# Reciprocals of the second MLP kept in SBUF, one block's input split later, keys split before queries

## The chip, the cores and the metric

The kernel runs on one core of a Trainium2 chip. The metric is the device time of one execution in microseconds (us). Runs of the kernel before are compared with runs of the changed kernel on the same chip.

## The reference, cut to what matters

An attention over 4 x 8 heads with 576 tokens and a head width of 64, masked by blocks of 64, is followed by two MLPs over 2304 tokens (model width 512, hidden width 2048):

```
x   = attention(q, k, v)                      # softmax over the blocks at or before one's own
x   = square(relu(x @ moe_w_in)) @ moe_w_out
h   = x @ moe2_w_in
P   = a[0] + a[1]*h + a[2]*h*h + a[3]*h*h*h
Q   = 1 + |b[0]|*|h| + |b[1]|*h*h
out = (P / (Q + 1e-6)) @ moe2_w_out
```

All arrays are float32.

## The kernel before, in words

**Precision.** TensorE multiplies in a rounded float32 format. Each factor is therefore kept as a high part (rounded) and a low part (the rest), and a product is three matmuls: high by high, low by high, high by low (PAIRS). High parts are written by a copy on ScalarE, low parts by a subtraction on VectorE or GpSimd (called POOL in the profile).

**Attention.** Heads 0 to 9 are multiplied plainly. Heads 10 to 31 are split: prep_qk (from line 249) runs one head ahead. In its first step ScalarE copies the scaled queries (qh, L259), then the keys (kk, L260). In the second step, one slot later, VectorE writes the queries' low part (L263, which reads qr and qh), POOL the keys' low part (L265, which reads kr and kk), and SP issues a DMA that copies the keys' high part to a second tile (L266). While the attention runs, TensorE fills in with the first half of the first MLP.

**First MLP.** Its hidden units are computed in halves; the second half of it runs after the attention, in units of one block of up to 512 tokens and 128 hidden columns.

**Second MLP** (from line 830). There are five blocks of tokens (512, 512, 512, 384, 384) and 16 slices of 128 hidden columns, so 80 units, 48 of width 512 and 32 of width 384. For unit u, TensorE multiplies x by a slice of w_in into a PSUM tile h (12 matmuls, L780; four such banks), and two units later g by a slice of w_out into the PSUM tiles yc (12 matmuls of 512 columns, 9 in the narrow blocks, L898), which are called down products here. Between them, with tiles t (three buffers), w and ab (two buffers each):

- ScalarE: ab = |h| (L878), w = c2*ab + c1 (L879), t = a3*h + a2 (L880)
- POOL: w = w*ab (L881); VectorE: t = h*t (L882), t = (t + a1)*h (L883)
- one unit later, ScalarE: ab = Ln of w (L862), r = Exp of -ab (L863), a first reciprocal of Q; VectorE: a Newton step and the product, w = (w + Q0)*r (L864), r = (2 - w)*r (L865), t = (t + a0)*r (L866)
- two units later, ScalarE writes g's high part from t (L857), POOL the low part (L858).

The tile r is chosen in L884: for the first two units (u < LAG) it is ab itself, in SBUF; for all others it is h, the PSUM tile of the unit, which is so read until L866. In the last two units VectorE takes POOL's part.

**What else runs there.** In units 0 to 9, split_late (L772 on ScalarE, L773 on POOL) splits the last ten of 16 late weight slices. The next block's x is split by split_x (L714 on ScalarE, L715 on POOL), in four pieces, at units 3, 5, 7 and 9 of a block.

**Order.** Tile's scheduler orders each engine's instructions when the kernel is built, by the program's order and a simulated timeline; on the chip each engine takes its queue in that order. tc.issue_after(x) ties what is issued in its block behind x on x's own engine. The lines that set the order around the change are these:

```
mid[u] = (ab, w, t, ab if u < LAG else h)                            # L884
if j + 1 < len(blocks3) and 3 <= m < 3 + 2 * KK and m % 2:           # L885
    with tc.issue_after(taken.ins), tc.issue_after(squared.ins):
        split_x(xt[j + 1], m // 2 - 1, blocks3[j + 1][1])
```

Of the kernel before, what the change touches and what calls it, by code (L numbers as in the profile page):

```python
# [11 lines left out]
AF = mybir.ActivationFunctionType  # L12
# [10 lines left out]
KK = DM // P  # L23
# [5 lines left out]
SCALE = 0.125  # L29
# [6 lines left out]
DOWN = 2.0 ** -63  # L36
# [8 lines left out]
def f(ap):  # L45
    return ap.bitcast(F32)
# [3 lines left out]
def attention_moe_moe(ctx: ExitStack, tc: tile.TileContext, q, k, v, wi1, wo1, wi2, wo2, a, b, out):  # L50
    nc = tc.nc
# [197 lines left out]
    def prep_qk(un, step):  # L249
        if un.plain:  # L250
            if step == 0 and un.scale == 1.0:
                cols = un.qr[:, un.q0:un.q1]
                nc.gpsimd.tensor_scalar(cols, cols, SCALE, 0.0, op0=ALU.mult, op1=ALU.add)
            return
        if step == 0:
            hd = un.hd
            un.qh = attn.tile([P, SP], F32R, tag="qh", name=f"qh{hd}", bufs=2)
            un.kk = attn.tile([P, S], F32R, tag="kk", name=f"kk{hd}", bufs=2)
            nc.scalar.activation(un.qh, un.qr, AF.Copy, scale=SCALE)  # L259
            nc.scalar.activation(un.kk, un.kr, AF.Copy)  # L260
        else:
            un.q2, un.k2 = q_two[un.hd % 2], k_two[un.hd % 2]
            nc.vector.scalar_tensor_tensor(  # L263
                un.q2[0:D], un.qr[0:D], SCALE, f(un.qh[0:D]), op0=ALU.mult, op1=ALU.subtract)
            nc.gpsimd.tensor_tensor(un.kk[D:P], un.kr[D:P], f(un.kk[D:P]), op=ALU.subtract)  # L265
            nc.sync.dma_start(f(un.k2[0:D]), f(un.kk[0:D]))  # L266
# [341 lines left out]
    lnb, exb = cab[:, 2:3], cab[:, 3:4]  # L608
# [35 lines left out]
    for i in range(NI + 5):  # L644
# [19 lines left out]
        if 0 <= i - 4 < NI:  # L664
            un, gi = slots[i - 4]
# [25 lines left out]
    def cut(small_first):  # L691
        tiles = NT // P
        nb = -(-tiles // (BLK // P))
        sizes = [P * (tiles // nb + (n < tiles % nb)) for n in range(nb)]
        cuts, t0 = [], 0
        for n in reversed(sizes) if small_first else sizes:
            cuts.append((t0, n))
            t0 += n
        return cuts

    blocks2, blocks3 = cut(True), cut(False)
# [10 lines left out]
    def split_x(xt, kk, n):  # L712
        hi, lo = xt[:, 0, kk, 0:n], xt[:, 1, kk, 0:n]
        nc.scalar.activation(hi, f(lo), AF.Copy)  # L714
        nc.gpsimd.tensor_tensor(lo, f(lo), f(hi), op=ALU.subtract)  # L715
# [69 lines left out]
    LAG = 2  # L785
# [5 lines left out]
    xt = {0: x_first}  # L791
    gs, ypart = {}, {}
    conv3.load()
    for u in range(len(units) + LAG):
        if u < len(units):
            j, m = units[u]
# [11 lines left out]
        if u >= LAG:  # L808
            j, m = units[u - LAG]
# [22 lines left out]
        at = u - (len(units) - HALF) - 1  # L832
# [10 lines left out]
    xt = {0: xt[len(blocks2)]}  # L843
    mid, gf = {}, {}
# [4 lines left out]
    for u in range(max(downs) + 1):  # L849
        if u - 2 in gf:  # L850
            t = gf.pop(u - 2)
            n = blocks3[units[u - 2][0]][1]
            if u - 2 >= final and (u - 2) % 7 > 2:
                g = half(len(blocks2) + len(blocks3))[:, :, (u - 2) % 7 - 3, 0:512]
            else:
                g = g2.tile([P, 2, 512], F32R, tag="g", name=f"gc{u - 2}", bufs=3)
            nc.scalar.activation(g[:, 0, 0:n], t, AF.Copy)  # L857
            (nc.vector if u - 2 >= len(units) - END else nc.gpsimd).tensor_tensor(g[:, 1, 0:n], t, f(g[:, 0, 0:n]), op=ALU.subtract)  # L858
            gs[u - 2] = g
        if u - 1 in mid:  # L860
            ab, w, t, r = mid.pop(u - 1)
            nc.scalar.activation(ab, w, AF.Ln, bias=lnb, scale=DOWN)  # L862
            nc.scalar.activation(r, ab, AF.Exp, bias=exb, scale=-1.0)  # L863
            nc.vector.scalar_tensor_tensor(w, w, Q0, r, op0=ALU.add, op1=ALU.mult)  # L864
            nc.vector.scalar_tensor_tensor(r, w, 2.0, r, op0=ALU.subtract, op1=ALU.mult, reverse0=True)  # L865
            nc.vector.scalar_tensor_tensor(t, t, a0, r, op0=ALU.add, op1=ALU.mult)  # L866
            gf[u - 1] = t
        split_late(u + len(blocks2) * HALF + LAG - SPLIT_AT, done)
        if u < len(units):
            j, m = units[u]  # L870
            t0, n = blocks3[j]
            if j + 1 < len(blocks3):
                if m == 0:
                    xt[j + 1] = load_x(xs2, *blocks3[j + 1], len(blocks2) + j + 1)
            ps = h_matmul(w3["i", m], xt[j], n, f"c{j}_{m}")
            h = ps[:, 0:n]
            ab, w, t = tmp("ab", n, f"ab{u}"), tmp("w", n, f"wq{u}"), tmp("t", n, f"t{u}")
            nc.scalar.activation(ab, h, AF.Abs)  # L878
            nc.scalar.activation(w, ab, AF.Identity, bias=c1, scale=c2)  # L879
            taken = nc.scalar.activation(t, h, AF.Identity, bias=a2, scale=a3)  # L880
            squared = (nc.vector if u >= len(units) - END else nc.gpsimd).tensor_tensor(w, w, ab, op=ALU.mult)  # L881
            nc.vector.tensor_tensor(t, h, t, op=ALU.mult)  # L882
            done = (taken, nc.vector.scalar_tensor_tensor(t, t, a1, h, op0=ALU.add, op1=ALU.mult))  # L883
            mid[u] = (ab, w, t, ab if u < LAG else h)  # L884
            if j + 1 < len(blocks3) and 3 <= m < 3 + 2 * KK and m % 2:  # L885
                with tc.issue_after(taken.ins), tc.issue_after(squared.ins):
                    split_x(xt[j + 1], m // 2 - 1, blocks3[j + 1][1])
        for v in downs.get(u, ()):
            j, m = units[v]
            t0, n = blocks3[j]  # L890
            g = gs.pop(v)
            for c in range(n // P):
                if m == 0:
                    acc[j, c] = psh.tile([P, 512], F32, tag="y", name=f"yc{j}_{c}", bufs=4)

                with tc.issue_after(last.ins) if c and v == len(units) - 1 else ExitStack():
                    for i, (zw, zg) in enumerate(PAIRS):
                        last = nc.tensor.matmul(acc[j, c], g[:, zg, P * c:P * (c + 1)], w3["o", m][:, zw, :],  # L898
                                                start=m == 0 and i == 0, stop=m == NM - 1 and i == 2)
                if m == NM - 1:  # L900
                    if c % 2 == 0:
                        o = g2.tile([P, 2, DM], F32, tag="wraw", name=f"o{j}_{c}", bufs=4)
                    y = acc.pop((j, c))
                    end_ = v == len(units) - 1 and c == n // P - 1
                    (nc.scalar.copy if c % 2 or end_ else nc.vector.tensor_copy)(o[:, c % 2], y)
                    if c % 2 or c == n // P - 1:
                        top = t0 + P * (c - c % 2)
                        (nc.scalar if end_ else nc.sync).dma_start(
                            out[top:t0 + P * (c + 1), :].rearrange("(a p) d -> p a d", p=P), o[:, 0:c % 2 + 1])
# [59 lines left out]
```

## Time and profile before

| | us |
|---|---|
| median of 3 runs | 1006.08 |
| lowest and highest of them | 1005.41, 1006.14 |
| the profiled execution | 1004.93 |
| its span, first to last instruction | 1003.2 |

The page of the profile gives, for the profiled execution, how long each engine was busy. PE is TensorE's matmul part, DVE is VectorE, ACT is ScalarE, SP issues DMAs. A time in the trace counts from the span's start. "Idle before" is how long the engine stood still ahead of an instruction, and the name behind "<-" is what it waited for. Lines are those of the kernel before. The time outside the span (1004.93 - 1003.2) belongs to no instruction.

### The profile page before, as it was taken

Reading aid. Unit: us, or ns where it says so; the run is one execution under the profiler, and the core shown is the slowest. Engines: PE = TensorE matmul, PEld = TensorE weight load, DVE = VectorE, ACT = ScalarE, POOL = GpSimd, SP = SyncE. Lnnn points to the kernel's source line nnn. Section 1 sums busy time; section 2 is a strip of 40 time slices with the busy share of each in tenths; the row PEclk is TensorE's granted clock in tenths of the full one; section 3 lists DMA queues with packets and bytes.
Section 4 is the critical chain, followed back from the end, with each engine's and each line's share of the span. In section 5 each row is a group of like instructions: output and inputs, shape, how many; then the busy total and the mean of one; then the engine's idle time right before and its main releaser. Section 6 shows DMA issues by size and latency. Waiting matters only on the chain.

```text
span 1003.2 us, 16323 instructions
## 1 busy us (share of the span) xinstructions
PE 992.0 (99%) x5361; PEld 864.6 (86%) x5361; DVE 724.8 (72%) x1389; ACT 723.8 (72%) x1590; POOL 570.5 (57%) x617
## 2 busy tenths in 40 slices
PE   8999999999999999999999999999999999999998
PEld 6678999888888899999888887888888888899997
DVE  7898687877787478767768766757666666666765
ACT  7888697887886467655455557867777777787885
POOL 5777597886787268421215386854655554555542
PEclk9999999999999999999999999999999999999999
DMA  9864334334332244569654651002001100200000
GB/s 295 267 198 149 114 113 132 89 106 130 105 107 83 97 131 124 207 184 300 230 191 151 231 157 58 1 1 84 1 1 32 42 1 1 74 1 1 32 1 32
DMA packets 63844, 106.67 MB, mean 106 GB/s; under 512 B 17040, under 2 KB 33424, under 8 KB 63760
## 3 DMA queue, kind: packets, MB, share of 16 engines
q1 hardware_dynamic: 63184, 105.05, 33.5%
q8 instruction: 42, 0.69, 0.3%
q10 hardware_dynamic: 576, 0.59, 0.2%
q14 instruction: 42, 0.34, 0.1%
HBM read 79.30 MB, written 23.07 MB: 102 GB/s over the span
## 4 chain that ended last, share of the span: by engine, by line
PE 91%; ACT 3%; DVE 2%; POOL 1%; DMA 1%; issue 1%; POOLq 0%; DVEq 0%; ACTq 0%; SPq 0%
PE yc L898 19%; PE hc L780 19%; PE hb L780 10%; PE yb L821 10%; PE ya L562 10%; PE ha L540 9%; PE tp L300 5%; PE pv L483 4%; PE sx L335 3%; PE sy L335 2%; PE pv L470 1%; DMA qr<-in_q_dram 1%; DMA raw_ai<-in_wi_dram 1%; POOL rb L387 0%; ACT p L371 0%
## 5 line engine op out<-in xcount | busy, mean ns | idle before, releaser
L780 PE MATMUL hc<-ring,w_ci 128*128 128x512 f32 (+1 forms) x960 | 210.2, 368 | 1.0 <-DVE t L866 1.0
L780 PEld LDWEIGHTS hc<-ring,w_ci 128*128 128x128 f32 x960 | 176.2, 188 | 27.0 <-DVE t L866 1.4
L898 PE MATMUL yc<-w_co,gc 128*128 128x512 f32 x792 | 191.7, 390 | 0.0
L898 PEld LDWEIGHTS yc<-w_co,gc 128*128 128x128 f32 x792 | 148.2, 188 | 29.3
L858 POOL TENSOR_TENSOR gc<-t,gc 128x512 fp32r<-128x512 f32 (+1 forms) x70 | 85.1, 1215 | 89.4 <-issue 61.0
L881 POOL TENSOR_TENSOR wq<-wq,ab 128x512 f32<-128x512 f32 (+1 forms) x78 | 92.8, 1190 | 75.0 <-ACT wq L879 74.7
L540 PE MATMUL ha<-ring,w_ai 128*128 128x512 f32 (+3 forms) x576 | 117.5, 348 | 0.5 <-DVE xp L487 0.5
L821 PE MATMUL yb<-gb,w_bo 128*128 128x512 f32 (+1 forms) x480 | 105.3, 367 | 0.0
L780 PE MATMUL hb<-ring,w_bi 128*128 128x512 f32 (+1 forms) x480 | 105.2, 367 | 0.0
L540 PEld LDWEIGHTS ha<-ring,w_ai 128*128 128x128 f32 x576 | 94.1, 189 | 11.3 <-issue 3.0
L715 POOL TENSOR_TENSOR ring<-ring 128x512 fp32r<-128x512 f32 (+1 forms) x40 | 52.4, 1311 | 88.0 <-ACT ring L714 83.2
L882 DVE TENSOR_TENSOR t<-hc,t 128x512 f32<-128x512 f32 (+1 forms) x80 | 50.9, 636 | 67.7 <-ACT t L880 67.7
L821 PEld LDWEIGHTS yb<-gb,w_bo 128*128 128x128 f32 x480 | 87.6, 188 | 11.4
L780 PEld LDWEIGHTS hb<-ring,w_bi 128*128 128x128 f32 x480 | 87.5, 188 | 11.1
L562 PE MATMUL ya<-gring,w_ao 128*128 128x352 f32 (+3 forms) x480 | 88.9, 331 | 0.0
L864 DVE SCALAR_TENSOR_TENSOR wq<-wq,hc 128x512 f32<-128x512 f32 (+1 forms) x78 | 49.3, 632 | 53.0 <-ACT hc L863 35.6
L300 PE MATMUL tp<-ident,p 128*128 128x128 f32 x480 | 82.1, 281 | 1.4 <-DVE stat L394 1.0
L562 PEld LDWEIGHTS ya<-gring,w_ao 128*128 128x128 f32 x480 | 75.9, 188 | 4.0 <-DVE s L578 0.2
L399 POOL TENSOR_SCALAR p<-p,stat 64x64 f32<-64x64 f32 (+4 forms) x110 | 60.3, 552 | 28.9 <-DVE stat L395 14.4
L443 DVE TENSOR_TENSOR pt<-tp,pt 128x128 fp32r<-128x128 f32 (+2 forms) x176 | 63.2, 391 | 18.6 <-ACT pt L441 11.9
L441 ACT ACTIVATE pt<-tp 128x128 fp32r<-128x128 f32 (+2 forms) x176 | 56.7, 365 | 19.3 <-PE tp L300 17.4
L878 ACT ACTIVATE ab<-hc 128x512 f32<-128x512 f32 (+1 forms) x80 | 44.2, 553 | 36.3 <-PE hc L780 36.0
(157 smaller groups left out, 2099.3 us busy)
## 6 DMA issues: line engine op xcount, KB each, us to landing
kr<-in_k_dram SPq DMA_DIRECT2D x32, 288.0 KB, 3.6
raw_ci<-in_wi_dram SPq DMA_DIRECT2D x16, 512.0 KB, 4.4
raw_co<-in_wo_dram SPq DMA_DIRECT2D x16, 512.0 KB, 4.0
qr<-in_q_dram SPq DMA_DIRECT2D x24, 320.0 KB, 3.2
ring<-xs SPq DMA_DIRECT2D x24, 256.0 KB, 4.2
raw_ai<-in_wi_dram SPq DMA_DIRECT2D x8, 512.0 KB, 5.2
raw_ao<-in_wo_dram SPq DMA_DIRECT2D x8, 512.0 KB, 4.6
raw_bi<-in_wi_dram SPq DMA_DIRECT2D x8, 512.0 KB, 3.9
```

The source lines that it names most:

```text
L300: yield nc.tensor.transpose(ps[:, P * n:P * (n + 1)], ptile(un, t)[:, P * c:P * (c + 1)], ident)
L399: nc.gpsimd.tensor_scalar(pv, pv, st[r:P, 6 + n:7 + n], 0.0, op0=ALU.mult, op1=ALU.add)
L441: nc.scalar.activation(high, src, AF.Copy)
L443: nc.vector.tensor_tensor(low, src, f(high), op=ALU.subtract)
L540: nc.tensor.matmul(ps[:, 0:n], w[:, zw, P * kk:P * (kk + 1)], ring[:, zx, kk, x0:x0 + n], start=i == 0, stop=i == 3 * KK - 1)
L562: nc.tensor.matmul(ps[c][:, 0:n], wA["o", m][:, zw, P * c:P * (c + 1)], gs[m][:, zg, 0:n], start=m == 0 and i == 0, stop=m == HALF - 1 and ...
L715: nc.gpsimd.tensor_tensor(lo, f(lo), f(hi), op=ALU.subtract)
L780: nc.tensor.matmul(ps[:, 0:n], w[:, zw, P * kk:P * (kk + 1)], xt[:, zx, kk, 0:n], start=i == 0, stop=i == 3 * KK - 1)
L821: nc.tensor.matmul(acc[j, c][:, 0:n], wB["o", m][:, zw, P * c:P * (c + 1)], g[:, zg, 0:n], start=m == 0 and i == 0, stop=last and i == 2)
L858: (nc.vector if u - 2 >= len(units) - END else nc.gpsimd).tensor_tensor(g[:, 1, 0:n], t, f(g[:, 0, 0:n]), op=ALU.subtract)
L881: squared = (nc.vector if u >= len(units) - END else nc.gpsimd).tensor_tensor(w, w, ab, op=ALU.mult)
L898: last = nc.tensor.matmul(acc[j, c], g[:, zg, P * c:P * (c + 1)], w3["o", m][:, zw, :], start=m == 0 and i == 0, stop=m == NM - 1 and i == 2)
```

## The change

It does three things. In prep_qk, ScalarE writes the keys' high part first and the queries' high part second, held in that order. In the second MLP, r is the ab tile in SBUF for all 80 units: Ln is written into it from w, Exp in place, and h is no longer written to. And the four splits of x for the second block move, within the first block, from units 3, 5, 7 and 9 to units 10 to 13; in later blocks they stay at 3, 5, 7 and 9.

```diff
--- before.py
+++ after.py
@@ -256,8 +256,9 @@
             hd = un.hd
             un.qh = attn.tile([P, SP], F32R, tag="qh", name=f"qh{hd}", bufs=2)
             un.kk = attn.tile([P, S], F32R, tag="kk", name=f"kk{hd}", bufs=2)
-            nc.scalar.activation(un.qh, un.qr, AF.Copy, scale=SCALE)
-            nc.scalar.activation(un.kk, un.kr, AF.Copy)
+            high = nc.scalar.activation(un.kk, un.kr, AF.Copy)
+            with tc.issue_after(high.ins):
+                nc.scalar.activation(un.qh, un.qr, AF.Copy, scale=SCALE)
         else:
             un.q2, un.k2 = q_two[un.hd % 2], k_two[un.hd % 2]
             nc.vector.scalar_tensor_tensor(
@@ -858,9 +859,9 @@
             (nc.vector if u - 2 >= len(units) - END else nc.gpsimd).tensor_tensor(g[:, 1, 0:n], t, f(g[:, 0, 0:n]), op=ALU.subtract)
             gs[u - 2] = g
         if u - 1 in mid:
-            ab, w, t, r = mid.pop(u - 1)
-            nc.scalar.activation(ab, w, AF.Ln, bias=lnb, scale=DOWN)
-            nc.scalar.activation(r, ab, AF.Exp, bias=exb, scale=-1.0)
+            r, w, t = mid.pop(u - 1)
+            nc.scalar.activation(r, w, AF.Ln, bias=lnb, scale=DOWN)
+            nc.scalar.activation(r, r, AF.Exp, bias=exb, scale=-1.0)
             nc.vector.scalar_tensor_tensor(w, w, Q0, r, op0=ALU.add, op1=ALU.mult)
             nc.vector.scalar_tensor_tensor(r, w, 2.0, r, op0=ALU.subtract, op1=ALU.mult, reverse0=True)
             nc.vector.scalar_tensor_tensor(t, t, a0, r, op0=ALU.add, op1=ALU.mult)
@@ -881,10 +882,11 @@
             squared = (nc.vector if u >= len(units) - END else nc.gpsimd).tensor_tensor(w, w, ab, op=ALU.mult)
             nc.vector.tensor_tensor(t, h, t, op=ALU.mult)
             done = (taken, nc.vector.scalar_tensor_tensor(t, t, a1, h, op0=ALU.add, op1=ALU.mult))
-            mid[u] = (ab, w, t, ab if u < LAG else h)
-            if j + 1 < len(blocks3) and 3 <= m < 3 + 2 * KK and m % 2:
+            mid[u] = (ab, w, t)
+            at = range(10, 14) if j == 0 else range(3, 11, 2)
+            if j + 1 < len(blocks3) and m in at:
                 with tc.issue_after(taken.ins), tc.issue_after(squared.ins):
-                    split_x(xt[j + 1], m // 2 - 1, blocks3[j + 1][1])
+                    split_x(xt[j + 1], at.index(m), blocks3[j + 1][1])
         for v in downs.get(u, ()):
             j, m = units[v]
             t0, n = blocks3[j]
```


## Rows read from the trace of the kernel before

**Rows 1.** The page, part 1: busy time, share and instructions of each engine.

```profile
PE 992.0 (99%) x5361; PEld 864.6 (86%) x5361; DVE 724.8 (72%) x1389; ACT 723.8 (72%) x1590; POOL 570.5 (57%) x617
```

**Rows 2.** Who waited for whom on PE: us in total, times, longest us.

```profile
PE tp L300 <- DVE stat L394: 1.0, 1, 1.0
PE hc L780 <- DVE t L866: 1.0, 1, 1.0
PE pv L483 <- ACT pt L441: 0.5, 2, 0.3
PE ha L540 <- DVE xp L487: 0.5, 1, 0.5
```

**Rows 3.** The chain of waits, two pieces: start us, us, what.

```profile
741.45 5.44 PE hc L780 x24
...
934.42 3.49 PE hc L780 x20
```

**Rows 4.** Timeline, 611 to 640 us: start, us, engine, line, op [idle before].

```profile
618.45 0.75 DVE L883 SCALAR_TENSOR_TENSOR t<-t,coef,hc 128x512 f32<-128x512 f32 x1
...
625.54 3.03 PE L780 MATMUL hc<-ring,w_ci 128*128 128x512 f32 x12 [0.97 <-DVE t L866]
...
627.68 1.30 POOL L858 TENSOR_TENSOR gc<-t,gc 128x512 fp32r<-128x512 f32 x1
```

**Rows 5.** Line 863 from 603 us on: duration ns min/median/max, first and last start.

```profile
L863 ACT ACTIVATE hc<-ab,cab x78: 567/690/697, 622.0 to 992.5; 128x512 f32<-128x512 f32 x46, 128x384 f32<-128x384 f32 x32
...
L863 ACT ACTIVATE ab<-ab,cab x2: 724/726/727, 611.4 to 613.5; 128x512 f32<-128x512 f32 x2
```

**Rows 6.** Lines 864 and 866 from 603 us on, the two units in SBUF.

```profile
L864 DVE SCALAR_TENSOR_TENSOR wq<-wq,ab x2: 683/844/1005, 612.3 to 614.7; 128x512 f32<-128x512 f32 x2
...
L866 DVE SCALAR_TENSOR_TENSOR t<-t,coef,ab x2: 752/1210/1669, 614.0 to 616.1; 128x512 f32<-128x512 f32 x2
```

**Rows 7.** Groups by shape, 626 to 1003.2 us: busy us, mean ns, idle before.

```profile
L858 POOL TENSOR_TENSOR gc<-t,gc 128x512 fp32r<-128x512 f32 x46 | 59.6, 1297 | 61.3 <-issue 38.6 <-ACT gc L857 20.0 <-PE yc L898 2.8
...
L866 DVE SCALAR_TENSOR_TENSOR t<-t,coef,hc 128x512 f32<-128x512 f32 x45 | 33.5, 745 | 1.0
...
L858 POOL TENSOR_TENSOR gc<-t,gc 128x384 fp32r<-128x384 f32 x22 | 22.4, 1018 | 25.2 <-issue 22.5 <-ACT gc L857 2.5
...
L866 DVE SCALAR_TENSOR_TENSOR t<-t,coef,hc 128x384 f32<-128x384 f32 x32 | 19.5, 610 | 0.6
```

**Rows 8.** Timeline again, 611 to 640 us: unit 0's low part and unit 1's L866.

```profile
615.52 1.74 POOL L858 TENSOR_TENSOR gc<-t,gc 128x512 fp32r<-128x512 f32 x1 [2.80 <-ACT gc L857]
...
616.14 1.67 DVE L866 SCALAR_TENSOR_TENSOR t<-t,coef,ab 128x512 f32<-128x512 f32 x1
```

**Rows 9.** Timeline again, 611 to 640 us: splits of x and of a late weight.

```profile
631.08 1.30 POOL L715 TENSOR_TENSOR ring<-ring 128x512 fp32r<-128x512 f32 x1 [0.51 <-ACT ring L714]
...
632.34 1.30 POOL L773 TENSOR_TENSOR w_ci<-w_ci 128x512 fp32r<-128x512 f32 x1
```

**Rows 10.** Timeline, 664 to 680 us: unit 11's low part and its down products.

```profile
669.98 1.30 POOL L858 TENSOR_TENSOR gc<-t,gc 128x512 fp32r<-128x512 f32 x1
...
673.74 2.88 PE L898 MATMUL yc<-w_co,gc 128*128 128x512 f32 x12
```

**Rows 11.** Timeline, 984 to 1003.2 us: the last three units.

```profile
992.63 6.28 PE L898 MATMUL yc<-w_co,gc 128*128 128x512 f32 x27
...
995.86 0.56 DVE L858 TENSOR_TENSOR gc<-t,gc 128x384 fp32r<-128x384 f32 x1 [0.59 <-ACT gc L857]
```

**Rows 12.** Timeline, 183 to 193 us, and line 263's durations: one head's split.

```profile
187.09 0.74 ACT L259 ACTIVATE qh<-qr 128x640 fp32r<-128x640 f32 x1
...
188.54 1.43 POOL L265 TENSOR_TENSOR kk<-kr,kk 64x576 fp32r<-64x576 f32 x1 [0.96 <-ACT kk L260]
188.56 2.09 DVE L263 SCALAR_TENSOR_TENSOR q_two<-qr,qh 64x640 fp32r<-64x640 f32 x1
...
L263 DVE SCALAR_TENSOR_TENSOR q_two<-qr,qh x22: 796/818/2087, 84.6 to 309.4; 64x640 fp32r<-64x640 f32 x22
```

## The prediction

> **What bounds the kernel now.** First the busy line of the page: TensorE (PE) is busy 992.0 of 1003.2 us, the other compute engines 570 to 725 [rows 1]. A full PE can still hold waits, so the table of waits on PE comes next: in the stretch of heads 10 to 31, where the edit of the keys lies, three entries make 1.0 + 0.5 + 0.5 = 2.0 us, and the whole second MLP has one, 1.0 us [rows 2]. The chain of waits shows the pace elsewhere: 24 matmuls of 512 columns in 5.44 us, 0.227 each, and 20 of 384 in 3.49, 0.175 each [rows 3]. So a unit of the second MLP (12 matmuls up, 12 or 9 down) costs PE 5.44 us at 512 tokens and 12 x 0.175 + 9 x 0.227 = 4.14 at 384. The change takes no matmul out, so it can win only those waits, 3.0 us at the most; it loses whenever the elementwise work of a unit, off the path today, comes later than PE wants it.
>
> **1. The h bank comes free earlier.** Unit 6's first matmul waits 0.97 us at 625.54 for L866 of unit 2, because r lies in unit 2's h bank. With r in SBUF the last reader of h is L883, which ended at 618.45 + 0.75 = 619.2 [rows 4]. The wait goes: 1.0 us gained. Late next is unit 2's low part, which POOL ends at 627.68 + 1.30 = 628.98 [rows 4]; until then PE can run units 6 and 7 up (2 x 2.72 us from 624.6, to 630.0), whose banks L883 also frees. So I take all of 1.0; the other end is nothing, if the queue's order puts unit 2's down products first.
>
> **2. Exp writes SBUF instead of PSUM.** The two units that do so already show the price: 0.726 us against 0.690 [rows 5], 0.04 x 78 on ScalarE, hidden under PE. Nothing in the sum. Ln in place is the same instruction.
>
> **3. VectorE and GpSimd get in each other's way.** This is the large unknown. L864 to L866 read r. From unit 2 on r is in PSUM today; in units 0 and 1 it is in SBUF, so both tensors they read are. There L864 took 0.683 and 1.005 us and L866 0.752 and 1.669, where L866 with its PSUM operand takes 0.745 on average [rows 6, 7]. The timeline shows why: POOL's L858 ran from 615.52 to 617.26, and L866, begun at 616.14, came out 0.55 us behind it; L858 itself took 1.74 where its mean is 1.30 [rows 7, 8]. So one waits for the other, and 1.12 + 0.75 - 1.67 = 0.20 us of a wait is made good. After the change all 80 units do this, three VectorE and two POOL instructions each. Shared time of a 512 unit: at most 3 x 0.745 on VectorE and, L881 taken like L858 (same shape, same kind), 2 x 1.297 on POOL, 4.83 us of PE's 5.44. Of a 384 unit: 3 x 0.61 + 2 x 1.02 = 3.87 of 4.14 [rows 7]. In units 0 to 9 the split of a late weight adds 1.30 on POOL, and in units 10 to 13 (after the third edit) a split of x adds 1.30 [rows 9]: 4.83 + 1.30 = 6.13. With three to four waits in a unit that each make good 0.20, that is 5.3 to 5.5, PE's own pace; the others fall to about 4.1 and 3.2. So POOL and VectorE keep up, barely in the first 14 units, and the cost is delay alone. A unit's chain grows by perhaps three waits of 0.3 to 0.9, 1.8 us, and one of POOL's of 0.45: 2.25. What covers it: in unit 11 POOL's low part is done at 671.28 and its down products begin at 673.74, 2.46 us later [rows 10]. In the last unit the low part ends at 995.86 + 0.56 = 996.42; its products are the last 9 of 27 from 992.63, the third begins at 992.63 + 20 x 0.227 = 997.17, and only 0.75 is spare [rows 11]. So 2.25 is hidden in the middle, and 2.25 - 0.75 = 1.5 shows at the end. The ends are nothing, if the waits fall into gaps, and 14 x (6.13 - 5.44) = 9.7 + 1.5 = 11.2, if nothing is made good. I take 1.5, nearest to the rows that show the spare.
> The Trainium skill ("SBUF — State Buffer", Who interferes with whom) speaks against this edit: a VectorE instruction with two SBUF inputs contends with a GpSimd instruction that reads SBUF, and the second to issue is blocked fully until the first is done. By that the end would be the 11.2; the trace agrees on who blocks, but shows the 0.20 made good.
>
> **4. A buffer is held longer.** r now lives in ab's buffer (two of them), so the Abs two units later waits for L866, not L863: up to three VectorE steps, 2.24 us [rows 7]. Behind it in ScalarE's queue stand that unit's two affine steps, and for those POOL's L881 waits. Mostly L857, which waits for the same L866, stands ahead of that Abs, and the spare of 2.46 us [rows 10] covers the rest: nothing, at most 2.2 once (a shift, not a loss per unit).
>
> **5. Block 0's x splits move** from units 3, 5, 7, 9 to 10 to 13: four ScalarE and four POOL instructions, no DMA. POOL is back to back from 631 to 634 [rows 9] and gains 1.3 us per split there. They are due at unit 16, whose products come at least two units (10.9 us) after unit 13's: nothing; with that cover gone unit 16 would wait.
>
> **6. Keys before queries on ScalarE**, 22 heads. POOL's L265 and SP's copy of the high part start some 0.7 us earlier (L259 takes 0.74), VectorE's L263 as much later. POOL stood 0.96 us idle for kk at 188.54; then L265 and L263 ran into each other, L263 took 2.09 us (its median is 0.82), and the transposes of that head waited 1.00 on VectorE [rows 2, 12]. With keys first L265 starts 0.7 earlier and L263's wait shrinks by as much. But where VectorE is free, it starts L263 today as ScalarE turns to kk, and POOL comes after; turned round, L263 can land on L265. I take 0.5 gained; the ends are 2.0 gained (all of PE's waits there) and 1.3 lost (one L263 of 2.09 for 0.82 on the path).
>
> **Sum:** -1.0 - 0.5 + 1.5 = 0, on the profiled execution's own 1004.9 us (span 1003.2); the median of the runs stands 1.15 above it, so 1004.9 + 1.15 = 1006.1. About 0.2% (2.0 us) is what a measurement of this kernel can tell from no change.
>
> **Rivals.** (a) **The sharing becomes the bound in units 0 to 13, slower.** There 6.13 us of shared time meet PE's 5.44. It decides once less than 0.69 us of a unit's waits is made good; then PE waits on the down products of these units, up to 14 x 0.69 = 9.7 us on top of the sum: 1015.8 in full, 1011 for half of it, 1008 for a fifth. For it: POOL runs without a gap there already [rows 9], so nearly every VectorE read of r meets it. Against: PE may run ahead on the banks freed earlier, and each split moved away gives POOL 1.3 us back in units 3 to 9. (That GpSimd blocks fully is the rule of the Trainium skill named above.) (b) **Both bubbles go and the waits fall into gaps, faster:** -1.0 - 2.0 = -3.0, 1003.1. For it: VectorE is a quarter idle. Against: every wait of three queues would have to vanish. (c) **The bank wait is only replaced:** the freed bank lets PE start unit 6, and it then waits as long for unit 2's low part at 628.98: 1006.1 + 1.0 = 1007.1, in effect no first edit.
>
> **Numbers.** Forecast 0.40, (a) 0.34, (b) 0.16, (c) 0.10. Forecast and (c) are within 2.0 us: same 0.50, slower 0.34, faster 0.16. The likeliest case alone: 1004.3 to 1008. Over all, from (b)'s edge at 1003.0 up to 1013.0, which leaves out about a third of (a) and the rest of (b), under 2 in 10.
>
> **What would show it.** Right: no wait of hc on L866 near 625; L866 longer on average (0.745 now), with single ones over 1.2; L858 and L881 above 1.30; PE still without waits from 690 to 860; a new wait of 1 to 2 us on the last units. Step 6: the idle of POOL before L265 falls, the wait at 191 is shorter. Wrong: PE waits on L857 or L858 in units 2 to 13 that add up to over 3 us, or the wait of 0.97 back under another releaser.

## The result, and the profile after

The changed kernel takes 1013.38 us in the median (1012.73 to 1013.56, 6 runs), the kernel before, on the same chip, 1005.35 us (1004.89 to 1006.14). The ratio is 1.0077, interval [1.0066, 1.0087]: 0.8% slower. The forecast was 1006.1 us with a range of 1003.0 to 1013.0, so the forecast missed and the range too, by 0.4 us. In the table below, one run of e12, at 5627.71 us and unexplained, is left out.

The page of the changed kernel: busy time of each engine.

```profile
PE 994.0 (98%) x5361; PEld 862.8 (85%) x5361; DVE 763.7 (76%) x1389; ACT 724.4 (72%) x1590; POOL 586.2 (58%) x617
```

Against [rows 1] VectorE has gained 39 us of busy time and GpSimd 16, with not one instruction more: the same instructions take longer. TensorE is busy 994 us, 2 more than before, in a span that is 8 us longer.

**Where the 8 us lie.** The stage of the split heads is read from the first matmul of keys by queries (sy, L335) to the last of probabilities by values (pv, L483); the second MLP from its first hc to its last yc. Instructions by tile, kernel before: duration in ns min/median/max, then the first and the last start in us.

```profile
L335 PE MATMUL sy<-kk,qh x66: 276/338/457, 90.6 to 330.2; 128*128 128x64 f32 x22, 128*128 128x192 f32 x22, 128*128 128x448 f32 x22
...
L483 PE MATMUL pv<-pt,vs x352: 220/282/395, 110.9 to 349.1; 128*128 128x256 f32 x110, 128*128 128x128 f32 x44, 128*128 128x320 f32 x22
...
L898 PE MATMUL yc<-w_co,gc x792: 387/389/402, 619.0 to 998.5; 128*128 128x512 f32 x198
...
L780 PE MATMUL hc<-ring,w_ci x960: 331/389/496, 599.9 to 988.3; 128*128 128x512 f32 x116, 128*128 128x384 f32 x76
```

The same of the changed kernel, whose lines stand one further down from L261 on and two from L885 on:

```profile
L336 PE MATMUL sy<-kk,qh x66: 276/336/457, 90.6 to 336.8; 128*128 128x64 f32 x22, 128*128 128x192 f32 x22, 128*128 128x448 f32 x22
...
L484 PE MATMUL pv<-pt,vs x352: 220/282/398, 110.8 to 355.6; 128*128 128x256 f32 x110, 128*128 128x128 f32 x44, 128*128 128x320 f32 x22
...
L900 PE MATMUL yc<-w_co,gc x792: 387/389/506, 625.5 to 1006.5; 128*128 128x512 f32 x198
...
L781 PE MATMUL hc<-ring,w_ci x960: 331/389/393, 606.5 to 996.3; 128*128 128x512 f32 x116, 128*128 128x384 f32 x76
```

The heads took 349.1 - 90.6 = 258.5 us and take 265.0: **6.5 us lost**. The first MLP's second half between them is untouched (349.1 to 599.9, and 355.6 to 606.5). The second MLP took 398.6 and takes 400.0: **1.5 us lost**. Together 8.0, the whole difference of the spans (1003.2 and 1011.1). So four fifths of the loss come from the edit that the prediction had put at a small gain.

**The heads.** Who waits for whom on TensorE, changed kernel, 85 to 350 us: total, times, longest.

```profile
PE tp L301 <- DVE stat L395: 4.1, 9, 0.8
PE pv L484 <- DVE stat L395: 1.0, 4, 0.3
PE pv L484 <- ACT pt L442: 0.7, 3, 0.2
PE pv L484 <- DVE stat L396: 0.7, 1, 0.7
```

Where one wait of the transposes on VectorE stood [rows 2], there are nine, and five more of pv on VectorE. These fourteen hang on VectorE's small steps L395 and L396, and at 5.8 us for the 1.0 of before they account for 4.8 of the 6.5 us; the rest shows in no long wait. What makes these late is in the timeline of a head. Of the kernel before, at 221 us (start, duration, instruction, [idle before]):

```profile
220.98 0.72 ACT L259 ACTIVATE qh<-qr 128x640 fp32r<-128x640 f32 x1
...
221.61 0.67 ACT L260 ACTIVATE kk<-kr 128x576 fp32r<-128x576 f32 x1
...
222.25 0.81 DVE L263 SCALAR_TENSOR_TENSOR q_two<-qr,qh 64x640 fp32r<-64x640 f32 x1
...
222.41 1.94 POOL L265 TENSOR_TENSOR kk<-kr,kk 64x576 fp32r<-64x576 f32 x1 [0.91 <-ACT kk L260]
```

And of the changed kernel, at 201 us:

```profile
200.77 0.67 ACT L259 ACTIVATE kk<-kr 128x576 fp32r<-128x576 f32 x1
...
201.34 0.73 ACT L261 ACTIVATE qh<-qr 128x640 fp32r<-128x640 f32 x1
...
202.09 1.43 POOL L266 TENSOR_TENSOR kk<-kr,kk 64x576 fp32r<-64x576 f32 x1
...
202.10 2.09 DVE L264 SCALAR_TENSOR_TENSOR q_two<-qr,qh 64x640 fp32r<-64x640 f32 x1
...
204.12 0.74 DVE L444 TENSOR_TENSOR pt<-tp,pt 128x384 fp32r<-128x384 f32 x2
...
204.79 0.13 DVE L395 TENSOR_SCALAR stat<-stat 128x1 f32<-128x1 f32 x1
...
205.00 0.52 PE L301 MATMUL tp<-ident,p 128*128 128x128 f32 x3 [0.76 <-DVE stat L395]
```

The two low parts met before, too, and one was held until the other was done. But the keys came second, GpSimd began second (0.16 us behind VectorE), and GpSimd was the one held: 1.94 us in place of 1.42, with nobody waiting. In the second timeline GpSimd begins first, if only by 0.01 us, and VectorE is held: 2.09 in place of 0.82. Behind it in VectorE's queue stand the copy of the transposes (L444) and the softmax's L395, and the next transposes wait for these. This head is the dearest; over the 22 heads GpSimd begins first in 20 (4 before), mostly by some 0.5 us. The durations in ns, min/median/max, of GpSimd's part before and of VectorE's in the changed kernel, which had a median of 818 [rows 12]:

```profile
L265 POOL TENSOR_TENSOR kk<-kr,kk x22: 1406/1588/2063, 84.5 to 309.6; 64x576 fp32r<-64x576 f32 x22
...
L264 DVE SCALAR_TENSOR_TENSOR q_two<-qr,qh x22: 809/1550/2094, 85.8 to 315.8; 64x640 fp32r<-64x640 f32 x22
```

Busy time of the 22 low parts, 80 to 330 us; L263 (queries) and L265 (keys) of the kernel before:

```profile
80.00:330.00 250.00, 23.12 (x22) 1.00 0.38 109
...
80.00:330.00 250.00, 36.66 (x22) 1.00 0.38 109
```

L264 (queries) and L266 (keys) of the changed kernel:

```profile
80.00:330.00 250.00, 32.37 (x22) 1.00 0.36 107
...
80.00:330.00 250.00, 32.51 (x22) 1.00 0.36 107
```

VectorE's parts take 9.3 us more, GpSimd's 4.2 less. The waiting has changed sides, from the engine that had time to the one that TensorE follows.

**The second MLP.** The wait of hc on L866 [rows 2, 4] is gone. Groups by shape of the changed kernel, from 606 us on (busy us, mean ns, idle before): two of the three steps that read r, and GpSimd's two.

```profile
L859 POOL TENSOR_TENSOR gc<-t,gc 128x512 fp32r<-128x512 f32 x48 | 70.5, 1476 | 83.0 <-ACT gc L858 41.3 <-issue 34.3 <-PE hc L781 6.4
L882 POOL TENSOR_TENSOR wq<-wq,ab 128x512 f32<-128x512 f32 x48 | 63.9, 1334 | 14.0 <-ACT wq L880 14.0
L867 DVE SCALAR_TENSOR_TENSOR t<-t,coef,ab 128x512 f32<-128x512 f32 x48 | 44.3, 924 | 1.1
L865 DVE SCALAR_TENSOR_TENSOR wq<-wq,ab 128x512 f32<-128x512 f32 x48 | 42.1, 876 | 24.6 <-ACT ab L864 12.9 <-POOL wq L882 11.3
```

L867 takes 924 ns on average where L866 took 745, and GpSimd's low part 1476 where it took 1297 [rows 7]. TensorE waits for that in units 10 to 18 alone. The longest of these waits, unit 12 (timeline, 682 to 690 us; its first line is unit 11's low part):

```profile
682.40 1.29 POOL L859 TENSOR_TENSOR gc<-t,gc 128x512 fp32r<-128x512 f32 x1
...
684.33 1.17 DVE L865 SCALAR_TENSOR_TENSOR wq<-wq,ab 128x512 f32<-128x512 f32 x1 [1.20 <-ACT ab L864]
...
685.53 1.67 DVE L866 SCALAR_TENSOR_TENSOR ab<-wq,ab 128x512 f32<-128x512 f32 x1
...
687.24 0.75 DVE L867 SCALAR_TENSOR_TENSOR t<-t,coef,ab 128x512 f32<-128x512 f32 x1
...
688.36 0.63 ACT L858 ACTIVATE gc<-t 128x512 fp32r<-128x512 f32 x1 [1.90 <-DVE t L867]
...
689.04 1.20 PE L900 MATMUL yc<-w_co,gc 128*128 128x512 f32 x4 [0.67 <-ACT gc L858]
```

Two of the unit's three steps met GpSimd (1.17 and 1.67 us where 0.69 is free), and the product began 0.67 us late. At the end, where the prediction had put the loss, there is none (timeline, 998 us on, the last products and the last low part, without a gap in TensorE's run):

```profile
1000.55 6.36 PE L900 MATMUL yc<-w_co,gc 128*128 128x512 f32 x27
...
1004.42 0.56 DVE L859 TENSOR_TENSOR gc<-t,gc 128x384 fp32r<-128x384 f32 x1 [0.59 <-ACT gc L858]
```

### The profile page after: what moved, and what is told of

Its sections match the earlier page's. It is cut to its first block, busy times and chain, and to the rows that moved or that the text cites. A ratio compares the mean times of both kernels' runs of the same rounds, so it can differ in the third digit from the quotient of the medians.

```text
span 1011.1 us, 16222 instructions
## 1 busy us (share of the span) xinstructions
PE 994.0 (98%) x5361; PEld 862.8 (85%) x5361; DVE 763.7 (76%) x1389; ACT 724.4 (72%) x1590; POOL 586.2 (58%) x617
## 4 chain that ended last, share of the span: by engine, by line
PE 75%; DVE 9%; ACT 7%; POOL 4%; issue 3%; DMA 1%; SPq 0%; DVEq 0%; ACTq 0%; POOLq 0%
PE yc L900 15%; PE hc L781 14%; PE hb L781 10%; PE yb L822 10%; PE ya L563 8%; PE ha L541 7%; PE tp L301 4%; PE pv L484 3%; PE sx L336 2%; PE sy L336 2%; DVE pt L444 2%; DVE q_two L264 1%; DVE stat L359 1%; DVE ab L866 1%; PE pv L471 1%
## 5 line engine op out<-in xcount | busy, mean ns | idle before, releaser
L900 PE MATMUL yc<-w_co,gc 128*128 128x512 f32 x792 | 194.2, 392 | 1.0 <-ACT gc L858 0.7
L900 PEld LDWEIGHTS yc<-w_co,gc 128*128 128x128 f32 x792 | 147.5, 188 | 32.3 <-ACT gc L858 1.8
L859 POOL TENSOR_TENSOR gc<-t,gc 128x512 fp32r<-128x512 f32 (+1 forms) x70 | 96.0, 1377 | 117.3 <-issue 65.4
L882 POOL TENSOR_TENSOR wq<-wq,ab 128x512 f32<-128x512 f32 (+1 forms) x78 | 94.5, 1213 | 24.4 <-ACT wq L880 23.3
L865 DVE SCALAR_TENSOR_TENSOR wq<-wq,ab 128x512 f32<-128x512 f32 (+1 forms) x80 | 62.6, 782 | 36.4 <-ACT ab L864 23.2
L858 ACT ACTIVATE gc<-t 128x512 fp32r<-128x512 f32 (+1 forms) x72 | 42.9, 595 | 61.0 <-DVE t L867 60.9
L444 DVE TENSOR_TENSOR pt<-tp,pt 128x128 fp32r<-128x128 f32 (+2 forms) x176 | 63.2, 391 | 15.1 <-ACT pt L442 7.9
```

The lines of the kernel that those rows point to most:

```text
L444: nc.vector.tensor_tensor(low, src, f(high), op=ALU.subtract)
```

## The experiments

All ratios are to the kernel before on the same chip. The stages are read as above; "queries' parts" is the busy time of VectorE's 22 low parts of the queries (not read where it is not used).

| run | median us (before) | ratio, interval | heads us | second MLP us | queries' parts us |
|---|---|---|---|---|---|
| kernel before | 1005.35 | | 258.55 | 398.59 | 23.1 |
| changed kernel | 1013.38 (1005.35) | 1.0077 [1.0066, 1.0087] | 265.07 | 400.05 | 32.4 |
| e1 keys first | 1011.76 (1005.89) | 1.0059 [1.0044, 1.0074] | 265.03 | 398.56 | 32.3 |
| e2 Exp in SBUF, splits moved | 1007.19 (1005.89) | 1.0009 [0.9999, 1.0019] | 258.60 | 400.09 | |
| e3 Exp in SBUF | 1007.13 (1005.89) | 1.0013 [1.0004, 1.0022] | 258.78 | 400.10 | |
| e4 splits moved | 1005.41 (1005.89) | 0.9999 [0.9989, 1.0008] | 258.87 | 398.05 | |
| e5 engines exchanged | 1013.55 (1005.50) | 1.0078 [1.0064, 1.0092] | 267.54 | 398.57 | |
| e6 queries' part twice | 1019.14 (1005.51) | 1.0135 [1.0119, 1.0152] | 269.85 | 398.62 | 59.0 (x44) |
| e7 Exp in SBUF, units 0 to 3 | 1007.97 (1005.50) | 1.0024 [1.0015, 1.0033] | 258.42 | 399.97 | |
| e8 keys first, no keys' part | 1007.27 (1005.50) | 1.0016 [1.0006, 1.0025] | 260.31 | 398.57 | 19.2 |
| e9 queries first, no keys' part | 1005.24 (1005.50) | 0.9999 [0.9990, 1.0008] | 257.99 | 398.60 | 17.9 |
| e10 keys first, copy between | 1011.49 (1005.51) | 1.0062 [1.0047, 1.0077] | 264.54 | 398.56 | 31.1 |
| e11 queries first, copy between | 1009.43 (1005.51) | 1.0035 [1.0022, 1.0048] | 260.88 | 398.61 | 23.5 |
| e12 keys first, in turn | 1006.50 (1005.56) | 1.0009 [0.9999, 1.0018] | 259.61 | 398.56 | 22.9 |
| e13 queries first, in turn | 1004.96 (1005.56) | 0.9989 [0.9980, 0.9998] | 257.93 | 398.56 | 21.3 |
| e14 Exp in SBUF from unit 20 | 1005.61 (1005.56) | 1.0002 [0.9992, 1.0011] | 258.65 | 398.60 | |
| e15 changed kernel, in turn | 1008.01 (1005.13) | 1.0034 [1.0020, 1.0047] | 259.51 | 400.04 | 22.8 |
| e16 e13 again | 1004.76 (1005.13) | 0.9997 [0.9988, 1.0006] | 257.94 | 398.56 | 21.3 |

### One edit at a time

**e1**: the kernel before with this edit alone.

```diff
-            nc.scalar.activation(un.qh, un.qr, AF.Copy, scale=SCALE)
-            nc.scalar.activation(un.kk, un.kr, AF.Copy)
+            high = nc.scalar.activation(un.kk, un.kr, AF.Copy)
+            with tc.issue_after(high.ins):
+                nc.scalar.activation(un.qh, un.qr, AF.Copy, scale=SCALE)
```

> Only the keys ahead of the queries on ScalarE. Theory A (the loss lies in the heads: VectorE's low part of the queries now lands on POOL's low part of the keys): the last attention product comes 6 to 7 us later than before and the kernel is 6 to 7 us slower. Rival B (the second MLP is what costs): within 1 us of before.

**e3**: the second edit alone.

```diff
-            ab, w, t, r = mid.pop(u - 1)
-            nc.scalar.activation(ab, w, AF.Ln, bias=lnb, scale=DOWN)
-            nc.scalar.activation(r, ab, AF.Exp, bias=exb, scale=-1.0)
+            r, w, t = mid.pop(u - 1)
+            nc.scalar.activation(r, w, AF.Ln, bias=lnb, scale=DOWN)
+            nc.scalar.activation(r, r, AF.Exp, bias=exb, scale=-1.0)
```

> Exp in SBUF, with block 0's splits left at units 3, 5, 7 and 9. If the sharing of SBUF by VectorE and POOL limits the first 14 units, the split work there adds to it early and PE waits sooner than with the splits moved: 2 to 6 us slower than before. If the sharing only delays single units, the same as with the splits moved, 1 to 2 us slower.

**e4**: the third edit alone; **e2**: the second and the third.

```diff
-            if j + 1 < len(blocks3) and 3 <= m < 3 + 2 * KK and m % 2:
+            at = range(10, 14) if j == 0 else range(3, 11, 2)
+            if j + 1 < len(blocks3) and m in at:
```

> Only block 0's splits at units 10 to 13, r in PSUM as before. Predicted at nothing: within 0.5 us of before, with the wait of 0.97 us of unit 6 still there, perhaps shorter, since POOL has one split less ahead of it.

> Only the second MLP's edits, Exp in SBUF and block 0's splits at units 10 to 13. Theory A: 1 to 2 us slower (its stage was 1.5 us longer in the changed kernel), the heads as before. Rival B: 6 us or more slower.

Measured: e1 loses 6.5 us in the heads and nothing elsewhere, e3 loses 1.5 us in the second MLP and nothing elsewhere, e4 changes the total by nothing that can be told from chance (in its trace the second MLP is 0.5 us shorter, as the bank wait is 0.4 in place of 1.0), and e2 is e3. The order on ScalarE carries 6.5 of the 8.0 us, the exponentials' place 1.5, the splits none of the loss.

### Is it the meeting of the two low parts?

**e8** and **e9** leave out GpSimd's low part of the keys, so that VectorE's part can meet nothing there; e8 writes the keys first, e9, the control, the queries first.

```diff
-            nc.gpsimd.tensor_tensor(un.kk[D:P], un.kr[D:P], f(un.kk[D:P]), op=ALU.subtract)
```

> Keys first, and POOL's low part of the keys left out (the scores lack that product). Theory A (the two low parts meet): without POOL's part nothing is met, VectorE's instruction is back at 0.82 us, and the time is within 1 us of the same kernel with queries first. Rival C (the queries' part starting 0.7 us later in VectorE's queue is what costs, whatever POOL does): still 5 us or more slower than with queries first.

> Queries first as before, and POOL's low part of the keys left out: the control for keys first without it. Theory A and rival C alike: at or up to 2 us below the kernel before, since POOL has 22 x 1.6 us less to do in a stretch where PE waits for only 2 us in all.

Measured: with the keys first the heads take 260.3 us, 4.7 less than with GpSimd's part (265.0); with the queries first 258.0, where that part costs 0.6. So the order by itself costs 260.3 - 258.0 = 2.3 us (theory A had allowed 1), and the other 4.2 of 6.5 need GpSimd's part.

The traces tell where these 2.3 us come from. With the keys first, Tile's scheduler also put other work in another order. In ten heads (11, 14, 19 to 21, 25 to 29, each from its first sy to the next head's) TensorE, VectorE, ScalarE and GpSimd start their instructions in e8 in e9's order but for the two copies; these heads take as long as in e9, to 0.02 us, though the queries' part starts one copy (0.6 us) later there too. All the 2.3 us lie in heads whose order differs. Between e8 and e1, on the other hand, the order on TensorE, VectorE and ScalarE is the same from head 11 on, and over these heads e1 is 5.2 us longer. So GpSimd's part costs that much with the three other queues as they were, and no new order of theirs is the reason.

**e5** writes the keys first and exchanges the engines: VectorE takes the keys' low part, which is ready first, and GpSimd the queries'.

```diff
+            high = nc.scalar.activation(un.kk, un.kr, AF.Copy, scale=SCALE)
+            with tc.issue_after(high.ins):
+                nc.scalar.activation(un.qh, un.qr, AF.Copy)
...
+            nc.vector.scalar_tensor_tensor(
+                un.kk[D:P], un.kr[D:P], SCALE, f(un.kk[D:P]), op0=ALU.mult, op1=ALU.subtract)
+            nc.gpsimd.tensor_tensor(un.q2[0:D], un.qr[0:D], f(un.qh[0:D]), op=ALU.subtract)
```

> Keys first, with the engines exchanged: VectorE writes the keys' low part, which is ready first, POOL the queries'; the scale moves from the queries' copy to the keys', a power of two. Theory A: the one instruction that comes first runs while ScalarE still copies the queries, as in the kernel before; the two no longer meet, and the time is within 1.5 us of before. Rival C, turned to keys: no loss either, as VectorE's part starts early. Rival D (keys first as such, by the order it gives the scheduler): 5 us or more slower still.

Measured: 1013.55 us, the heads 267.5: longer than in the changed kernel. Theory A missed (1.5 us at most), and the number is the one that rival D named (5 us or more). Line 264 of this run, duration in ns min/median/max:

```profile
L264 DVE SCALAR_TENSOR_TENSOR kk<-kr,kk x22: 748/756/2173, 84.1 to 318.8; 64x576 fp32r<-64x576 f32 x22
```

VectorE is no longer held as a rule (median 756 ns), yet in a few heads, where it comes to its part late, the two begin in the same 0.01 us and it is held for 2.17. Three such heads make TensorE wait 1.4, 1.1 and 1.4 us, and the stage loses more than by the changed kernel's many short waits. The last of them (timeline, 284 to 292 us):

```profile
284.19 1.55 POOL L266 TENSOR_TENSOR q_two<-qr,qh 64x640 fp32r<-64x640 f32 x1
284.20 2.17 DVE L264 SCALAR_TENSOR_TENSOR kk<-kr,kk 64x576 fp32r<-64x576 f32 x1
...
287.59 0.33 PE L484 MATMUL pv<-pt,vs 128*128 128x128 f32 x1 [1.40 <-DVE stat L395]
...
288.88 3.41 PE L541 MATMUL ha<-ring,w_ai 128*128 128x512 f32 x9
```

After its 1.40 us of waiting TensorE takes 3.41 / 9 = 0.38 us for a matmul of 512 columns that takes 0.227 elsewhere [rows 3], as its granted clock had fallen (windows around that wait; granted clock is the column behind the busy times):

```profile
280.00:286.00 6.00, 5.77 (x33) 4.62 (x31) 5.84 (x11) 5.14 (x15) 4.93 (x7) 1.00 0.30 85
286.00:292.00 6.00, 4.60 (x19) 3.80 (x18) 4.87 (x18) 2.77 (x11) 4.65 (x7) 0.72 0.39 127
292.00:298.00 6.00, 6.00 (x37) 5.30 (x36) 4.23 (x8) 4.80 (x11) 4.11 (x6) 1.00 0.21 52
```

So this run does not speak against the meeting, but shows that it matters who is held, and that each of the two waits of 1.4 us was followed by a stretch at the lower clock. It does not prove it either: it changed too much at once. Rival D is answered by e8, where the keys come first as well and only 2.3 us are lost.

**e6** keeps the queries first and writes VectorE's part twice, one behind the other.

```diff
             nc.vector.scalar_tensor_tensor(
                 un.q2[0:D], un.qr[0:D], SCALE, f(un.qh[0:D]), op0=ALU.mult, op1=ALU.subtract)
+            nc.vector.scalar_tensor_tensor(
+                un.q2[0:D], un.qr[0:D], SCALE, f(un.qh[0:D]), op0=ALU.mult, op1=ALU.subtract)
```

> The kernel before (queries first) with VectorE's low part of the queries written twice, one behind the other: 22 times 0.8 us or more of VectorE work at the place where the change lengthens it, ScalarE's order unchanged. Theory A (TensorE's steps hang on VectorE's queue right behind that place): the stage of the split heads grows by 2 to 6 us, total 1008 to 1012 us, with the same new waits of TensorE on VectorE's stat of L394 and its neighbours. Rival C (VectorE has room there, and it is the order on ScalarE itself that costs): the stage stays within 1 us of 258.55, total 1005 to 1006.5 us.

Measured: 1019.14 us; the heads take 269.85, 11.3 more and twice what theory A allowed for. TensorE's waits, with the lines two further down than before:

```profile
PE tp L302 <- DVE stat L396: 6.7, 8, 1.1
PE pv L485 <- DVE stat L396: 3.5, 7, 0.5
```

VectorE's two sets of parts take 59.0 us where one took 23.1, so 11.3 of 35.9 us, a third, come through to TensorE. (The scheduler's order of other work differs here in most heads, and the figure holds that too.) VectorE is busy for 191 of 255 us in this stage of the kernel before (90 to 345 us) and still has no room at this place. The same waits as in the changed kernel arise without exchanging ScalarE's copies.

### The two parts in turn

**e10** and **e11** were to make GpSimd wait until VectorE's part is done, by a small copy ahead of GpSimd's subtraction (e10 keys first, e11 queries first).

```diff
+            turn_ = attn.tile([P, 8], F32, tag="turn", name=f"turn{un.hd}", bufs=2)
+            nc.gpsimd.tensor_scalar(turn_[0:D], f(un.q2[0:D, 0:8]), 1.0, 0.0, op0=ALU.mult, op1=ALU.add)
             nc.gpsimd.tensor_tensor(un.kk[D:P], un.kr[D:P], f(un.kk[D:P]), op=ALU.subtract)
```

> The kernel before with the keys written first, and with GpSimd's low part of the keys made to wait until VectorE's low part of the queries is done (GpSimd first copies 8 columns of that result into a scratch tile): the same work, the same order on ScalarE, but the two low parts no longer run at once. Theory A (it is the meeting of the two that costs, and it costs because VectorE is the one that is held): the 22 queries' low parts fall from 32.3 us to 18 to 20, the stage of the split heads falls from 265.0 us to 259 to 261 (as without GpSimd's part, 260.3), total 1006 to 1008 us. Rival B (a late low part on GpSimd holds back its next work, as the mirrored version seemed to say): the queries' low parts fall as well, but the stage stays at 264 us or more, total 1010 us or more, with waits for GpSimd's results (p of L400, ring) on TensorE.

> The kernel before (queries first) with the same turn: GpSimd's low part of the keys waits for VectorE's low part of the queries. Theory A: the 9 stretched queries' low parts become short (22 take 18 us in place of 23.1), TensorE's wait of 1.0 us near 191 us goes, the stage of the split heads takes 257.5 to 258.5 us in place of 258.55, total 1004.0 to 1005.5 us: a gain of 0 to 1.2 us. Rival B (lateness on GpSimd costs): the stage takes 259.5 us or more, total 1006.5 us or more.

Measured: neither did what it was to do, and neither says anything on the theory. Nothing tied the subtraction to the copy, and the scheduler queued it ahead; e10's queries' parts still take 31.1 us. e10 is e1 with 22 copies of 0.2 us more, and as slow. e11 loses 2.3 us in the heads; 1.2 of it lie in the first split head, where the scheduler put TensorE's products of the first MLP in another order, and the rest stays unexplained.

**e12** and **e13** tie the subtraction behind the copy in GpSimd's queue.

```diff
+            seen = nc.gpsimd.tensor_scalar(turn_[0:D], f(un.q2[0:D, 0:8]), 1.0, 0.0, op0=ALU.mult, op1=ALU.add)
+            with tc.issue_after(seen.ins):
+                nc.gpsimd.tensor_tensor(un.kk[D:P], un.kr[D:P], f(un.kk[D:P]), op=ALU.subtract)
```

> Keys written first; GpSimd copies 8 columns of VectorE's low part of the queries, and its own low part of the keys now stands behind that copy in its queue (in the run before it, that copy had been queued behind the low part, and the two low parts still met). Theory A (VectorE is held by a low part that GpSimd began first): none of the 22 queries' low parts meets the keys', their sum falls from 32.3 us to 18 to 22, the stage of the split heads takes 259 to 261.5 us, total 1006 to 1008.5 us. Rival B (whatever stands between the keys' part and VectorE's later work, the stage loses 6 us): the sum falls all the same, the stage takes 264 us or more, total 1010.5 us or more.

> Queries first, as in the kernel before, with the same order on GpSimd's queue. Theory A: the queries' low parts sum to 18 to 20 us in place of 23.1, the wait of 1.0 us near 191 us goes, the stage of the split heads takes 257.8 to 258.8 us, total 1004.5 to 1006 us. Rival B: GpSimd's part now starts 0.3 us or more later in each head, the stage takes 260 us or more, total 1007 us or more.

Measured: e12's heads take 259.6 us, e13's 257.9, both where theory A had put them; the sums of the queries' parts, 22.9 and 21.3 us, are some 1 us above the bounds given, as in several heads VectorE's part met other work of GpSimd (1.83 us at 200.48, beside its L583). One head of e12 (timeline, 222 to 226 us):

```profile
222.96 0.82 DVE L264 SCALAR_TENSOR_TENSOR q_two<-qr,qh 64x640 fp32r<-64x640 f32 x1
223.87 0.20 POOL L267 TENSOR_SCALAR turn<-q_two 64x8 f32<-64x8 f32 x1 [1.57 <-DVE q_two L264]
...
224.14 1.41 POOL L269 TENSOR_TENSOR kk<-kr,kk 64x576 fp32r<-64x576 f32 x1
```

Each takes its undisturbed time, GpSimd's part ends at 225.55, and nobody waits for it. All the work of e1 is there, GpSimd's lies even later, and 5.4 of the 6.5 us are gone. Of the 5.4, 3.2 lie in heads where TensorE, VectorE and ScalarE keep e1's order. So the meeting is the cause of some 5 us, 5.4 by this run and 5.2 by e8. The keys' coming first without a meeting, e12 against e13, costs 1.7, near the 2.3 of e8 against e9, which were the scheduler's new order.

### The second MLP

**e7** moves r to SBUF for units 2 and 3 as well, and no further.

```diff
-            mid[u] = (ab, w, t, ab if u < LAG else h)
+            mid[u] = (ab, w, t, ab if u < 4 else h)
```

> The kernel before with r in SBUF for the first four units instead of two. Unit 6's wait of 0.97 us for the bank of unit 2 goes; six more VectorE instructions meet POOL, in units whose down products have some slack: 0.5 to 1 us faster than before. If the sharing delays units 2 and 3 past their down products, PE waits there instead and the time is the same.

Measured: a miss. Unit 6's wait goes, but a longer one comes at unit 8, for the bank that unit 4 holds in PSUM: 2.4 us, at 638.5 us.

```profile
PE hc L780 <- DVE t L866: 2.4, 1, 2.4
```

Of the six steps of units 2 and 3 on VectorE three take 1.67 us, and unit 4's L866, which frees the bank, begins 4.6 us later in the stage than before. The stage loses about what the whole edit loses (399.97 against 398.59 us), with two units of 78, but by another wait: in the changed kernel no bank is held until that step.

**e14** puts r in SBUF from unit 20 on and leaves units 2 to 19 in PSUM.

```diff
+            mid[u] = (ab, w, t, ab if u < LAG or u >= 20 else h)
```

> The kernel before with the exponentials in SBUF for units 0, 1 and from unit 20 on, and in PSUM for units 2 to 19 (the splits of x unmoved, queries first). Theory C (the dearer units cost only where VectorE still pays off the work of the first units, up to some unit 18): the second MLP takes 398.4 to 398.9 us, as before, with the wait of 1.0 us of hc near 625 us back, total 1005 to 1006.3 us. Rival D (the loss is spread over the units, or lies at the last ones): 399.5 us or more, total 1006.8 us or more.

Measured: 398.60 us, as before, and the wait of 0.9 us on hc is back. 60 units in SBUF cost nothing; the 1.5 us come from units 2 to 19.

### Together, and the best version

**e15** is the changed kernel with e12's order, **e16** is e13 in more rounds.

> The whole changed kernel, with GpSimd's low part of the keys queued behind a copy from VectorE's low part of the queries. If the two losses are separate and add up: the split heads take 259.6 us as in the run with the keys first and the parts in turn, the second MLP 400.05 us as in the changed kernel, so 5.5 us of its 8.0 us go and the total is 1007 to 1009 us (the changed kernel: 1013.4). If the loss in the second MLP were an echo of the late heads, it would fall to 398.6 us and the total to 1005.5 to 1006.5 us.

> The run with queries first and the two low parts in turn once more, in more rounds: 0.5 to 0.6 us below the kernel before (ratio 0.9990 to 0.9998) if its gain was real, within 0.0004 of 1 if it was chance.

Measured: e15's heads fall to 259.5 us, its second MLP stays at 400.04, so the two losses are separate and add up. e16 gives 0.9997, interval [0.9988, 1.0006], after 0.9989 [0.9980, 0.9998]: both medians lie 0.4 to 0.6 us below the kernel before, and both profiled heads at 257.9 us in place of 258.55, but the second interval holds 1. Whether e13 beats the kernel before can't be said; it is no worse, and beats the changed kernel by 8 us.

## Why the prediction was wrong

**Step 6, keys before queries, failed**: "I take 0.5 gained; the ends are 2.0 gained and 1.3 lost (one L263 of 2.09 for 0.82 on the path)". It cost 6.5 us. The mechanism was there, "turned round, L263 can land on L265", and so was the price of one meeting, 1.3 us. What failed is the bound: it counted one such L263 on the path where the edit touches 22 heads. ScalarE's order decides in most heads who begins first, so the bound had to be 22 times what one costs, 22 x 1.27 = 28 us, and rows of before could have narrowed it: GpSimd's part took 1588 ns in the median and up to 2063 there, against 1406 undisturbed, so GpSimd was held in about half of the heads, and that cost nothing. Per head the change costs 6.5 / 22 = 0.30 us, for 0.42 us more of VectorE's part (9.3 / 22). What the step described came about: GpSimd's part starts earlier, and the wait of 1.00 us near 191 us is down to 0.37 (at 193.19). What it did not ask is who pays when the two meet in the other heads, and whether the exchange leaves the other queues in their order, which it did not.

The bound could look small because VectorE seemed to have room ("a quarter idle", rival (b)). Of the time added at this place a third reached TensorE in e6 (11.3 of 35.9 us), and more than half in e1 against e12 (5.4 of 9.4).

**Step 3, the sharing of SBUF**, had the right mechanism, the right order and the wrong place. Taken were 1.5 us at the last units. The second MLP lost 1.5 us on balance, and as the bank wait of 1.0 went, the dearer steps cost 2.4. None of it is at the end; it is in units 10 to 18 (6 to 18 in e3), where the spare of 2.46 us was taken from unit 11 of the kernel before [rows 10]. The step took a unit's delay of 2.25 us as one that stays in its unit, but it adds up from unit to unit: counted from the stage's first hc (599.93 and 606.47 us), unit 11's low part was done at 71.35 us and is done at 77.22 in the changed kernel, 5.9 later, and the spare is gone. That unit's last hc matmul begins 4.9 us earlier, at 55.98 for 60.89. As the traces read, the bank wait had kept TensorE from running ahead of the elementwise work; with the banks free sooner and that work slower, the first units' backlog lasts to unit 18. No run tested this account by itself; e14 shows only that the loss comes from units 2 to 19. Steps of TensorE longer than the median of their shape, from one start to the next, add up to 2.7 us between 675 and 725 us, against nothing before.

The Trainium skill ("SBUF — State Buffer", Who interferes with whom) has a VectorE instruction with two SBUF inputs contend with a GpSimd instruction that reads SBUF, and the second to issue blocked fully until the first is done. The changed kernel agrees but for 0.15 us: at 202.09 us GpSimd took 1.43, and VectorE, begun 0.01 later, 2.09, where 1.42 of waiting and 0.82 of work make 2.24.

**Step 1** was right in what goes: the wait of hc is no longer there. "I take all of 1.0" was too much, as the time came back as waits on the down products; e7 shows what can come in its place. **Step 2** was right (0.725 us a piece, hidden), **step 5** too (e4: 0.9999; its trace shows a gain of 0.5 us, too little for the times to tell), and **step 4** was not separated: what it costs, if anything, is in e3's 1.5 us and in the 2.4 above.

**The rivals.** Rival (a) named 1008 to 1015.8 us and the time fell there, but by luck: its mechanism, waits of TensorE on the down products, came about in units 10 to 18 and is worth the 2.7 us above, and the whole second MLP lost 1.5 us; the other 6.5 are step 6's. (c), the bank wait replaced, gives that stage the 1.5 us that it lost (1.0 above the forecast), but not at the place that it named, unit 2's low part, for which nothing waits. No rival was made of step 6, since its bound was small. That is why the range ended at 1013.0.

## What to carry to other kernels

When two engines hold each other up in SBUF, list the pairs of their instructions that run at about the same time, and ask which begins first: the other one pays, and a swap of two inputs can move that payment from an engine with slack to the one that TensorE follows. Bound such a swap by the number of places where it acts, not by the one place where it showed. Compare the engines' orders before and after as well: the scheduler can answer a swap of two instructions by moving others (here some 2 us). A wait on TensorE may be what gives the other engines their spare, so the spare has to be taken from a trace without it.

## What the runs showed of the hardware

- Who is held is decided by starts 0.01 us apart (202.09 and 202.10: VectorE held for 1.3 us), and some of the wait is made good: 0.15 us there, and at 222.41, where GpSimd is held, 222.25 + 0.81 + 1.42 - 224.35 = 0.13.
- In e5 a wait of 1.40 us on TensorE was followed by a granted clock of 0.72 over 6 us, so part of that stretch at 1.2 GHz in place of 2.4, and so was its other wait of 1.40, which ended at 195.80 (0.79 over 194 to 202 us); its wait of 1.12, which ended at 208.20, was not (1.00 over 205 to 213 us). The changed kernel's waits of up to 0.76 us left it at 1.00 (204 to 208 us). The length of a wait alone does not decide: a wait of 1.07 us was followed by 0.50 over 23.3 to 26.5 us in e11 (it ended at 23.18), and by 1.00 over the same stretch in the kernel before (it ended at 22.63).
